# Reordering the seven products of a Strassen-Winograd multiplication, and multiplying by h straight from the accumulator

## The chip, the core and the metric

The kernel runs on one core of one Trainium2 chip. The metric is the device time of one execution in microseconds, as a median over runs; it includes what lies around the instructions of the program. The profile comes from one more execution under the hardware profiler. Its page gives the span from the first to the last instruction, and the times in the profile count from the start of that span.

## The reference

An attention block feeds a feed-forward block. For each of 8 batches, with 8 heads of 64 columns, 512 tokens read 32 states and the 32 states read the 512 tokens. The results of all batches are stacked into 4352 rows of 512 columns, and the feed-forward block turns each row into a row of 512 again, through 2048 hidden columns.

```python
scores = scale * np.matmul(x, state.transpose(0, 1, 3, 2))
a = softmax(scores);  xread = np.matmul(a, state)           # 512 rows a batch
scores2 = scale * np.matmul(state, x.transpose(0, 1, 3, 2))
a2 = softmax(scores2); sread = np.matmul(a2, x)             # 32 rows a batch
x = concatenate([xread, sread], axis=2) -> (4352, 512)
h = x @ w_in                                                # 512 x 2048
g = h * erf(softplus(h))
out = g @ w_out                                             # 2048 x 512
```

The two weights arrive as 64-bit numbers and are made into 32-bit ones on the chip.

## The kernel before

**The weights.** Each weight comes in 8 pieces (`i` for w_in, `o` for w_out). A piece is loaded as raw words into one of three buffers by a DMA of the SyncE queue, then ScalarE makes two steps of its conversion (L152, L154) and VectorE three (L155, L156, L157); the last VectorE step also issues the DMA of the third piece after it. This goes on through the whole first batch.

**The first batch.** For batch 0 the hidden columns are worked through in four groups g of 512 columns, each in four parts i of 128. `mixed_part` (L455) multiplies the states with a piece of w_in into m (copied from the accumulator by ScalarE, L457 and L458). `first0` (L828) multiplies m with the attention weights into a tile h of the accumulator, PSUM. h then goes two ways: `soft` (ScalarE, L832) writes softplus(h) into `gT[0]`, and `keep_h` (VectorE, L835) copies h into `gT[1]`. `erf` (ScalarE, L838) works on `gT[0]` in place, `times` (VectorE, L841) multiplies `gT[0]` with the copy in `gT[1]`, and `some0` or `by_halves` multiply the result with w_out (`project`, L626). ScalarE loads a new function table each time it goes from softplus to erf or exp and back.

[...] The pool `ps_h` holds two (tiles `h`), `ps_at` two (tiles `at`, used by `mixed_part`, by the scores and by transposes), `ps_o` four (tiles `o`, the sums of the second multiplication). A tile is given again only when its readers are done.

**The other batches.** Batches 1 to 7 are worked through in 14 turns n = 0 to 13, two for each batch b (u = 0 and 1, each for half of the hidden columns). Here each of the two multiplications of the feed-forward block is done as a 2 x 2 block product with seven multiplications instead of eight, with sums of blocks made before and after (Winograd's form). `hidden_wide` makes the first multiplication (L559, adds of VectorE in L542, copies of ScalarE in L565 and L574, softplus in L552). `erf_part` and `finish_on_act` (L1082, L616) and `times_part` (L1086) finish g. `sums_of` makes the sums S1 to S4 of its blocks on VectorE (L734, L735), and `combine_w` those of w_out, T1 to T4 (L652).

`project_wide` is the second multiplication, and the place of the first part of the change. One call of it is a pass: seven products, each four matmuls of 256 columns (the profile shows each matmul as two records, so a product has 8). It has two banks, p and q, in halves: a and d are the halves of p, c and e those of q. Before, the seven come in this order, with the adds of VectorE (L686) and the copies of ScalarE (L707, L719) between them:

| product | into | what follows it |
|---|---|---|
| A11 B11 | a | ScalarE copies a to m1 |
| S2 T2 | c | u2 = m1 + c |
| S1 T1 | d | v = u2 + d |
| S3 T3 | c, afresh | o2 = (u2, v) + (c, c) |
| A12 B21 | a, added to | ScalarE copies a to c11, a half of o1 |
| A22 T4 | e | c21 += e (a half of o2), o2 is stored |
| S4 B22 | d, afresh | c12 = v + d (a half of o1), o1 is stored |

A turn has two passes. The inner one runs by itself after the hidden stage of its turn. The outer one is kept as `pending`: its first half-products are laid between the products of the next turn's `hidden_wide`, which gives VectorE and ScalarE time there, and the rest follows that stage. A pass yields after each half of a product and after each product; the number k of the yield decides what else is put there. At k = 5 stands the excursion: reading the tokens of a batch (L285), the mixed weights of the next (`mixed_pair`, L442) and the scores of the one after (L205). `after` (the two `times_part` of the outer half) stands at k = 3, and in turns 4, 6, 8 and 10 the exps of the next batch's softmax (L388, L390 on ScalarE) stand at k = 5 too. `fill` and `rest` deal out smaller jobs of VectorE.

**The order.** Each engine works through its instructions in the order in which the program gives them, which is fixed by `in_order`. An instruction waits on semaphores until what it reads is there and what it overwrites has been read.

Of the kernel before, what the change touches and what calls it, by code (L numbers as in the profile page):

```python
# [9 lines left out]
F32 = mybir.dt.float32  # L10
U32 = mybir.dt.uint32
ALU = mybir.AluOpType
# [5 lines left out]
def kernel(  # L18
# [40 lines left out]
    outs = ctx.enter_context(tc.tile_pool(name="outs", bufs=2))  # L59
# [285 lines left out]
    def all_of(jobs):  # L345
        for f in jobs:
            f()
# [283 lines left out]

    def store(acc, put):
        for r in range(NC):
            ot = outs.tile([P, d_model], F32, name="ot")
            nc.scalar.copy(ot, acc[r])
            put(r, ot)

    E2 = d_model // 2
# [41 lines left out]
    def project_wide(n, g, put, more):  # L680
        gT, hs = slot(n)
        blocks = lambda t: [t[:, k].rearrange("p (i t) -> p i t", i=GF) for k in range(4)]
        A11, A21, A12, A22 = blocks(gT)
        S1, S2, S3, S4 = blocks(hs)
        tt = nc.vector.tensor_tensor
        add = lambda o, x, y: tt(o, x, y, op=ALU.add)  # L686
        half = n_acc[0] % 2
        n_acc[0] += 1
        p, q = (ps_o.tile([P, d_model], F32, name="o%d" % (2 * half + k)) for k in range(2))
        halves = lambda t: (t[:, 0:E2], t[:, E2:])  # L690
        (a, d), (c, e) = halves(p), halves(q)
        m1 = outs.tile([P, E2], F32, name="m1")
        uv = outs.tile([P, d_model], F32, name="uv")
        o1, o2 = (outs.tile([P, d_model], F32, name="ot") for _ in range(2))
        (c11, c12), (c21, c22), (u2, v) = halves(o1), halves(o2), halves(uv)
        two = lambda t: t.rearrange("p (c e) -> p c e", c=2)

        def product(lhs, rhs, out, start=False):
            for i in range(GF):
                if i == 2:  # L700
                    yield
                nc.tensor.matmul(out=out, lhsT=lhs[:, i, :], rhs=rhs[:, g, i, :],  # L702
                                 start=(start and i == 0), stop=(i == GF - 1),
                                 skip_group_check=not start)

        yield from product(A11, B11, a, True)
        nc.scalar.copy(m1, a)  # L707
        yield
        yield from product(S2, T[2], c, True)
        add(u2, m1, c)  # L710
        yield
        yield from product(S1, T[1], d)
        add(v, u2, d)
        yield
        yield from product(S3, T[3], c, True)
        add(two(o2), two(uv), c.unsqueeze(1).to_broadcast([P, 2, E2]))
        yield
        yield from product(A12, B21, a)
        nc.scalar.copy(c11, a)  # L719
        yield  # L720
        yield from product(A22, T[4], e)
        add(c21, c21, e)
        put(1, o2, more=more)
        yield
        yield from product(S4, B22, d, True)
        add(c12, v, d)
        put(0, o1, more=more)

    def sums_of(n):
# [9 lines left out]
    def store7(acc, put):  # L739
        twice = lambda t: t.unsqueeze(1).to_broadcast([P, 2, E2])  # L740
        two = lambda t: t.rearrange("p (c e) -> p c e", c=2)
        m1 = outs.tile([P, E2], F32, name="m1")
        u3 = outs.tile([P, d_model], F32, name="uv")[:, 0:E2]
        o1, o2 = (outs.tile([P, d_model], F32, name="ot") for _ in range(2))
# [34 lines left out]
    def begins(b):  # L779
        return 1 - b % 2  # L780
# [42 lines left out]
    h_t = {}  # L823

    def first0(g, i, gT):
        h = h_t[i] = ps_h.tile([P, S], F32, name="h")
        for e in range(2):
            nc.tensor.matmul(out=h, lhsT=m_t[0, g][:, e, P * i:P * i + P], rhs=aT[0][:, e],  # L828
                             start=(e == 0), stop=(e == 1))

    def soft(i, gT):
        nc.scalar.activation(out=gT[0][:, i], in_=h_t[i], func=ACTF.Softplus)  # L832

    def keep_h(i, gT):
        nc.vector.tensor_copy(gT[1][:, i], h_t[i])  # L835

    def erf(ks, gT):
        nc.scalar.activation(out=gT[0][:, ks], in_=gT[0][:, ks], func=ACTF.Erf)  # L838

    def times(ks, gT):  # L840
        nc.vector.tensor_tensor(gT[0][:, ks], gT[0][:, ks], gT[1][:, ks], op=ALU.mult)  # L841

    groups = [0]

# [27 lines left out]
    def some0(g, gT, rs, ts):  # L872
        done(project(gT[0], g, acc, rs, ts))

    def evict(i, gT, late=False):
        for f in (keep_h, soft) if late else (soft, keep_h):
            f(i, gT)
# [7 lines left out]
    keep_h(0, g0)  # L885
    on_dve("o", 0, [1])
    soft(1, g0)
    keep_h(1, g0)
    mixed_part(0, 0, 1, 2, nc.scalar.copy, nc.scalar.copy)
    on_dve("o", 0, [2])  # L890
    erf(A, g0)
# [1 line left out]
    on_act("o", 1)  # L893
    for i in 2, 3:
        first0(0, i, g0[0])
        evict(i, g0, True)
    erf(Z, g0)
    acc = tiles(NC)
    some0(0, g0, range(NC), range(2))
# [12 lines left out]
    g1 = group()  # L912
    first0(1, 0, g1[0])
    on_dve("o", 2, [0])
    evict(0, g1, True)
# [4 lines left out]
    evict(1, g1, True)  # L920
    on_act("o", 3, [1])
    on_dve("o", 3, [0])
    erf(A, g1)
    on_act("i", 4)
    first0(1, 2, g1[0])
    keep_h(2, g1)
    on_dve("o", 3, [1])
    first0(1, 3, g1[0])
    times(A, g1)
    keep_h(3, g1)  # L930
    on_dve("o", 3, [2])
    some0(0, g0, range(2, 3), range(3, 4))
    some0(0, g0, range(3, 4), range(2, 4))
# [16 lines left out]
    g2 = group()  # L950
    first0(2, 0, g2[0])
    on_dve("o", 4, [0, 1])
    evict(0, g2, True)
    mixed_part(0, 2, 1, 2, nc.scalar.copy, nc.scalar.copy)
    first0(2, 1, g2[0])
    on_act("o", 5, [0])
    evict(1, g2, True)
    on_dve("o", 4, [2])
    on_act("o", 5, [1])
    first0(2, 2, g2[0])  # L960
    evict(2, g2, True)
    on_dve("o", 5, [0])
    first0(2, 3, g2[0])
    evict(3, g2, True)
    on_dve("o", 5, [1])
    some0(1, g1, range(1, 4), range(2, 4))

# [30 lines left out]
    mixed_part(0, 3, 1, 2, nc.scalar.copy, nc.scalar.copy)  # L998
    first0(3, 1, g3[0])
    soft(1, g3)  # L1000
    all_of(most[:6])
    for i in 0, 1:
        keep_h(i, g3)
    all_of(most[6:])
    exps()
    on_dve("o", 6, [2])
# [1 line left out]
    some0(2, g2, range(1, 2), range(2, 4))  # L1008
    for i in 2, 3:
        first0(3, i, g3[0])  # L1010
        evict(i, g3)
    some0(2, g2, range(2, 3), range(2, 4))
    finish_(g3)
    mixed(1, 2 * begins(1), nc.scalar.copy, nc.scalar.copy)
    some0(2, g2, range(3, 4), range(2, 4))
    all_of(ready[:4])
    on_act("o", 7)
# [6 lines left out]
    def by_halves():  # L1024
        yield from project(g3[0], 3, acc, range(NC), range(2))
        for r in range(NC):
            yield from project(g3[0], 3, acc, range(r, r + 1), range(2, 4))
            ot = outs.tile([P, d_model], F32, name="ot")
            nc.scalar.copy(ot, acc[r])
            put_x(0, r // 2)(r % 2, ot)  # L1030

# [62 lines left out]
    for n, (b, u) in enumerate((b, u) for b in range(1, B) for u in range(2)):  # L1094
# [45 lines left out]
        for k, _ in enumerate(steps):  # L1140
            k += 6
            if k == 6:
                fill(1.2)
            if k == 7:
                fill(1.2)
            if k == 8 and n == 2:
                excursion(2, m_next, 3)
                bring(1 - begins(b + 1))
            if k == 9:
                break  # L1150
# [30 lines left out]
        def rest(n):  # L1181
            for _ in range(min(n, len(more))):
                more.popleft()()

        for k, _ in enumerate(project_wide(inner, o, put[1 - low], u)):
            if k == 0:
                all_of(sums[3:])
                fill(0.6)
            if k == 3:
                all_of(after)  # L1190
            if k == 4:
                fill(99)
            if k == 5 and n != 2:
                if b == 1:
                    excursion(m=m_next)
                elif u == 0:
                    excursion(m=m_next)
                else:
                    excursion(b + 1 if b + 1 < B else None, m_next, b + 2 if b + 2 < B else None)
                if u == 0 and b + 1 < B:  # L1200
                    bring(1 - begins(b + 1))
                if b == B - 1 and u == 0:
                    for i in range(0, B, 4):
                        turn_read(range(i, min(i + 4, B)))
                if steady and u == 0 and b + 1 < B:
                    soft[b + 1][1]()
            rest({5: 1 if n == 2 or b == B - 1 else 4 if u else 3, 6: 1, 7: 0, 8: 2, 9: 1, 10: 2, 11: 1, 12: 1}.get(k, 0))
        if n > 1:
            rest(99)
# [60 lines left out]
```

## Time and profile before

| | |
|---|---|
| time, median of 3 runs (lowest to highest) | 729.69 us (729.67 to 730.13) |
| time of the profiled execution | 729.88 us |
| its span | 728.0 us |
| TensorE, matmuls: busy | 716.6 us, 98% |
| TensorE, weight loads: busy | 562.0 us, 77% |
| VectorE busy | 546.0 us, 75% |
| ScalarE busy | 370.1 us, 51% |
| granted clock of TensorE | 1.000 |
| share of the chain that ended last: TensorE, ScalarE, VectorE | 80%, 4%, 3% |
| copies of h in the first batch (L835) | 16, 685 ns each |
| multiplications by the copy (L841) | 4 of 1024 columns, 1223 ns; 8 of 512 columns, 685 ns |
| adds of the seven products (L686) | 112 of 256 columns, 415 to 421 ns; 28 of 512, 680 ns |
| copies of the seven products (L707, L719) | 28 and 28, 364 and 361 ns |

A row of the timeline has the start and the duration in us, the engine, the line, the operation, the tiles written and read, and how many records are merged in it; the brackets say how long the engine had been idle and what released it. PE is TensorE, PEld its weight loads, DVE VectorE, ACT ScalarE, POOL GpSimd, SPq the DMA queue of SyncE. In the table by stage the columns after each pair of times are the busy times of PE, PEld, DVE, ACT and POOL with their instructions, then the granted clock, the DMA share and GB/s. Matmuls overlap in the pipeline, so that their busy times say less than the distance between their starts.

### The profile page before, as it was taken

The page shows a single profiled execution, that of the slowest core. Times are in us where ns is not written, and L with a number is a line of the kernel's source. Part 1 is how long each engine was busy: PE and PEld are TensorE (multiplying, and loading weights), DVE is VectorE, ACT ScalarE, POOL GpSimd, SP SyncE. Part 2 cuts the span into 40 slices and gives each one's busy share as a digit, 9 for nine tenths or more (in the row PEclk, how much of TensorE's full clock was granted, in tenths as well). Part 3 has the DMA queues.
Part 4 walks back from the last instruction along what each step waited for, and adds up shares of the span by engine and source line. Part 5 has one row for each costly group of instructions (what it writes and reads, how often), then busy time and mean ns, then how long its engine had stood idle before and what let it go on. Part 6 is the DMA issues. An engine that isn't in the chain of part 4 may idle for free.

```text
span 728.0 us, 10875 instructions
## 1 busy us (share of the span) xinstructions
PE 716.6 (98%) x4232; PEld 562.0 (77%) x4232; DVE 546.0 (75%) x872; ACT 370.1 (51%) x536; POOL 25.2 (3%) x34
## 2 busy tenths in 40 slices
PE   8899999999999999999999999999999999999997
PEld 7434436588778878887888878787888888889996
DVE  4988899788868998678776867698777756765533
ACT  4898894536354534645345526453464434342340
POOL 0000000000100000000000000000000000000000
PEclk9999999999999999999999999999999999999999
DMA  7587786560239154422714270614232231102201
GB/s 235 175 244 216 217 235 232 145 181 30 38 65 215 48 123 65 98 86 67 128 18 155 54 138 14 174 26 128 50 81 102 71 67 19 40 30 30 23 7 29
DMA packets 142907, 74.64 MB, mean 103 GB/s; under 512 B 127112, under 2 KB 127368, under 8 KB 141320
## 3 DMA queue, kind: packets, MB, share of 16 engines
q1 hardware_dynamic: 136552, 65.89, 32.8%
q0 software_dynamic: 4032, 7.34, 7.6%
q10 hardware_dynamic: 2272, 0.72, 0.5%
q8 instruction: 33, 0.54, 0.3%
q14 instruction: 18, 0.15, 0.1%
HBM read 49.81 MB, written 20.45 MB: 97 GB/s over the span
## 4 chain that ended last, share of the span: by engine, by line
PE 80%; ACT 4%; DVE 3%; issue 1%; ACTq 0%; DVEq 0%
PE o L702 44%; PE h L559 13%; PE at L559 10%; PE h L604 3%; PE o L676 3%; PE h L442 2%; PE at L442 1%; ACT xT L390 1%; PE at L285 1%; PE o L626 1%; PE h L205 1%; DVE ring L1086 0%; DVE w_out L156 0%; ACT ring L838 0%; ACT ring L1082 0%
## 5 line engine op out<-in xcount | busy, mean ns | idle before, releaser
L702 PE MATMUL o<-w_out,ring 128*128 128x256 f32 x896 | 209.5, 381 | 0.4
L702 PEld LDWEIGHTS o<-w_out,ring 128*128 128x128 f32 x896 | 168.4, 190 | 35.6 <-DVE uv L686 5.5
L702 PE MATMUL o<-raw,ring 128*128 128x256 f32 x672 | 161.3, 380 | 1.3 <-DVE ring L734 0.7
L702 PEld LDWEIGHTS o<-raw,ring 128*128 128x128 f32 x672 | 127.1, 190 | 19.9 <-issue 1.1
L552 ACT ACTIVATE ring<-ring 128x512 f32<-128x512 f32 x112 | 70.6, 631 | 61.5 <-DVE ring L542 60.9
L1086 DVE TENSOR_TENSOR ring<-ring 128x1024 f32<-128x1024 f32 x60 | 71.8, 1221 | 20.9 <-ACT ring L1082 16.9
L559 PE MATMUL h<-aT,m 128*128 128x256 f32 x336 | 82.2, 380 | 0.1
L559 PEld LDWEIGHTS h<-aT,m 128*128 128x128 f32 x336 | 63.5, 190 | 11.0 <-DVE ring L542 1.2
L542 DVE TENSOR_TENSOR ring<-ring,at 128x512 f32<-128x512 f32 x84 | 57.0, 679 | 14.8 <-PE at L559 13.1
L626 PE MATMUL o<-w_out,ring 128*128 128x512 f32 x128 | 59.0, 599 | 0.6 <-DVE ring L841 0.5
L542 DVE TENSOR_TENSOR ring<-ring,h 128x512 f32<-128x512 f32 x56 | 37.9, 676 | 22.8 <-PE h L559 21.0
L686 DVE TENSOR_TENSOR ot<-uv,o 128x512 f32<-128x512 f32 (+1 forms) x56 | 30.7, 549 | 27.2 <-PE o L702 24.7
L565 ACT COPY ring<-h 128x512 f32<-128x512 f32 x28 | 16.4, 586 | 64.0 <-PE h L559 64.0
L762 POOL DMA_DIRECT2D out_dram<-ot x28 | 24.5, 936 | 663.4 <-DVE ot L686 663.4
L626 PEld LDWEIGHTS o<-w_out,ring 128*128 128x128 f32 x128 | 23.5, 190 | 29.4 <-issue 24.4
L574 ACT COPY ring<-h 128x512 f32<-128x512 f32 x28 | 16.4, 588 | 47.0 <-PE h L559 47.0
L734 DVE TENSOR_TENSOR ring<-ring 128x512 f32<-128x512 f32 x56 | 38.6, 689 | 1.4
L735 DVE TENSOR_TENSOR ring<-ring 128x512 f32<-128x512 f32 x56 | 36.2, 683 | 0.0
L828 PE MATMUL h<-aT,m 128*128 128x512 f32 x64 | 29.8, 604 | 1.0 <-ACT m L457 0.5
L616 ACT ACTIVATE ring<-ring 128x2048 f32<-128x2048 f32 x16 | 30.5, 1905 | 0.0
L444 ACT COPY m<-h 128x512 f32<-128x512 f32 x11 | 6.4, 586 | 46.7 <-PE h L442 46.7
L1082 ACT ACTIVATE ring<-ring 128x1024 f32<-128x1024 f32 x28 | 29.6, 1059 | 0.2
(180 smaller groups left out, 955.4 us busy)
## 6 DMA issues: line engine op xcount, KB each, us to landing
w_in<-kept_in SPq DMA_DIRECT2D x7, 2048.0 KB, 8.5
raw<-in_moe_w_in_dram SPq DMA_DIRECT2D x8, 1024.0 KB, 5.7
raw<-in_moe_w_out_dram SPq DMA_DIRECT2D x8, 1024.0 KB, 4.9
out_dram<-ot SPq DMA_DIRECT2D x32, 256.0 KB, 2.2
xq<-in_x_dram SPq DMA_DIRECT2D x112, 64.0 KB, 2.3
x<-in_x_dram SPq DMA_DIRECT2D x56, 128.0 KB, 2.8
out_dram<-ot POOLq DMA_DIRECT2D x28, 256.0 KB, 4.5
sc<-xT SPq DMA_DIRECT2D x112, 32.0 KB, 1.9
```

Of the source, the lines that this page charges most:

```text
L542: add = lambda o, x, y: nc.vector.tensor_tensor(o, x, y, op=ALU.add)
L552: nc.scalar.activation(out=s[k], in_=hs[k], func=ACTF.Softplus)
L559: nc.tensor.matmul(out=out[:, i], lhsT=x[:, q:q + P], rhs=y, start=(first and i == 0), stop=(i == 1), skip_group_check=not first)
L616: nc.scalar.activation(out=s, in_=s, func=ACTF.Erf)
L626: nc.tensor.matmul(out=acc[r], lhsT=gT[:, i, P * r:P * r + P], rhs=w_out[:, GF * g + i, :], start=(g == 0 and i == 0), stop=(g == NG - 1 a ...
L686: add = lambda o, x, y: tt(o, x, y, op=ALU.add)
L702: nc.tensor.matmul(out=out, lhsT=lhs[:, i, :], rhs=rhs[:, g, i, :], start=(start and i == 0), stop=(i == GF - 1), skip_group_check=not start)
L734: return [lambda: tt(S1, A21, A22, op=ALU.add), lambda: tt(S2, S1, A11, op=ALU.subtract), lambda: tt(S3, A11, A21, op=ALU.subtract), lambd ...
L735: lambda: tt(S3, A11, A21, op=ALU.subtract), lambda: tt(S4, A12, S2, op=ALU.subtract)]
L828: nc.tensor.matmul(out=h, lhsT=m_t[0, g][:, e, P * i:P * i + P], rhs=aT[0][:, e], start=(e == 0), stop=(e == 1))
L1082: nc.scalar.activation(out=s[:, ks], in_=s[:, ks], func=ACTF.Erf)
L1086: nc.vector.tensor_tensor(s[:, ks], s[:, ks], hs[:, ks], op=ALU.mult)
```

## The change

First, the seven products of `project_wide` stand in another order, and two sums are formed in another way. A22 T4 becomes the second product. S3 T3 is added to S2 T2 in the accumulator and S4 B22 to S1 T1, where both started afresh before. A12 B21 and the copy of c11 close the pass. c12 is begun already after S2 T2, in the output tile. m1 moves into the tile `uv`, and the output tiles `ot` have three buffers instead of two. Some numbers k move with it: the exps of the later turns to k = 7, the excursion of turn 2 to k = 7 of its pending pass, and in turn 2 six steps of the next softmax stand at k = 3 and `after` at k = 10.

Second, in the first batch `keep_h` is gone: h stays in PSUM until `times` multiplies with it, one part i at a time. The third and fourth h of a group are tiles of `ps_at`. The first `mixed` of batch 1 moves from behind group 3's erf to ahead of the softmax steps of batch 1.

```diff
@@ store, project_wide
-        m1 = outs.tile([P, E2], F32, name="m1")
         uv = outs.tile([P, d_model], F32, name="uv")
-        o1, o2 = (outs.tile([P, d_model], F32, name="ot") for _ in range(2))
-        (c11, c12), (c21, c22), (u2, v) = halves(o1), halves(o2), halves(uv)
+        o1, o2 = (outs.tile([P, d_model], F32, name="ot", bufs=3) for _ in range(2))
+        (c11, c12), (c21, c22), (m1, v) = halves(o1), halves(o2), halves(uv)
...
         yield from product(A11, B11, a, True)
         nc.scalar.copy(m1, a)
         yield
-        yield from product(S2, T[2], c, True)
-        add(u2, m1, c)
+        yield from product(A22, T[4], e, True)
+        yield
+        yield from product(S2, T[2], c)
+        add(c12, m1, c)
         yield
         yield from product(S1, T[1], d)
-        add(v, u2, d)
+        add(v, m1, d)
         yield
-        yield from product(S3, T[3], c, True)
+        yield from product(S3, T[3], c)
         add(two(o2), two(uv), c.unsqueeze(1).to_broadcast([P, 2, E2]))
         yield
+        yield from product(S4, B22, d)
+        yield
         yield from product(A12, B21, a)
-        nc.scalar.copy(c11, a)
-        yield
-        yield from product(A22, T[4], e)
         add(c21, c21, e)
         put(1, o2, more=more)
-        yield
-        yield from product(S4, B22, d, True)
-        add(c12, v, d)
+        nc.scalar.copy(c11, a)
+        add(c12, c12, d)
         put(0, o1, more=more)
@@ the first batch
     def first0(g, i, gT):
-        h = h_t[i] = ps_h.tile([P, S], F32, name="h")
+        pool, name = ((ps_h, "h"), (ps_at, "at"))[i // 2]
+        h = h_t[i] = pool.tile([P, S], F32, name=name)
...
-    def keep_h(i, gT):
-        nc.vector.tensor_copy(gT[1][:, i], h_t[i])
-
     def times(ks, gT):
-        nc.vector.tensor_tensor(gT[0][:, ks], gT[0][:, ks], gT[1][:, ks], op=ALU.mult)
+        for i in range(ks.start, ks.stop):
+            nc.vector.tensor_tensor(gT[0][:, i], gT[0][:, i], h_t[i], op=ALU.mult)
...
     soft(1, g3)
+    mixed(1, 2 * begins(1), nc.scalar.copy, nc.scalar.copy)
     all_of(most[:6])
-    for i in 0, 1:
-        keep_h(i, g3)
     all_of(most[6:])
     exps()
...
     finish_(g3)
-    mixed(1, 2 * begins(1), nc.scalar.copy, nc.scalar.copy)
     some0(2, g2, range(3, 4), range(2, 4))
@@ the turns
-            if k == 8 and n == 2:
+            if k == 7 and n == 2:
                 excursion(2, m_next, 3)
...
             if k == 3:
+                if n == 2:
+                    rest(6)
+                else:
+                    all_of(after)
+            if k == 10 and n == 2:
                 all_of(after)
...
-                if steady and u == 0 and b + 1 < B:
-                    soft[b + 1][1]()
+            if k == 7 and steady and u == 0 and b + 1 < B:
+                soft[b + 1][1]()
```

More of the change, by code (lines that the diff above doesn't have):

```diff
@@ L633, in store @@
         for r in range(NC):
-            ot = outs.tile([P, d_model], F32, name="ot")
+            ot = outs.tile([P, d_model], F32, name="ot", bufs=3)
             nc.scalar.copy(ot, acc[r])
@@ L741, in store7 @@
         two = lambda t: t.rearrange("p (c e) -> p c e", c=2)
-        m1 = outs.tile([P, E2], F32, name="m1")
-        u3 = outs.tile([P, d_model], F32, name="uv")[:, 0:E2]
-        o1, o2 = (outs.tile([P, d_model], F32, name="ot") for _ in range(2))
+        uv = outs.tile([P, d_model], F32, name="uv")
+        m1, u3 = uv[:, 0:E2], uv[:, E2:]
+        o1, o2 = (outs.tile([P, d_model], F32, name="ot", bufs=3) for _ in range(2))
         c12 = o1[:, E2:]
@@ L873, in some0 @@
         done(project(gT[0], g, acc, rs, ts))
-    def evict(i, gT, late=False):
-        for f in (keep_h, soft) if late else (soft, keep_h):
-            f(i, gT)
     first0(0, 0, g0[0])
@@ L884 @@
     on_dve("o", 0, [0])
-    keep_h(0, g0)
     on_dve("o", 0, [1])
     soft(1, g0)
-    keep_h(1, g0)
     mixed_part(0, 0, 1, 2, nc.scalar.copy, nc.scalar.copy)
@@ L895 @@
         first0(0, i, g0[0])
-        evict(i, g0, True)
+        soft(i, g0)
     erf(Z, g0)
@@ L914 @@
     on_dve("o", 2, [0])
-    evict(0, g1, True)
+    soft(0, g1)
     mixed_part(0, 1, 1, 2, nc.scalar.copy, nc.scalar.copy)
@@ L919 @@
     on_act("o", 3, [0])
-    evict(1, g1, True)
+    soft(1, g1)
     on_act("o", 3, [1])
@@ L925 @@
     first0(1, 2, g1[0])
-    keep_h(2, g1)
     on_dve("o", 3, [1])
@@ L929 @@
     times(A, g1)
-    keep_h(3, g1)
     on_dve("o", 3, [2])
@@ L952 @@
     on_dve("o", 4, [0, 1])
-    evict(0, g2, True)
+    soft(0, g2)
     mixed_part(0, 2, 1, 2, nc.scalar.copy, nc.scalar.copy)
@@ L956 @@
     on_act("o", 5, [0])
-    evict(1, g2, True)
+    soft(1, g2)
     on_dve("o", 4, [2])
@@ L960 @@
     first0(2, 2, g2[0])
-    evict(2, g2, True)
+    soft(2, g2)
     on_dve("o", 5, [0])
     first0(2, 3, g2[0])
-    evict(3, g2, True)
+    soft(3, g2)
     on_dve("o", 5, [1])
@@ L1010 @@
         first0(3, i, g3[0])
-        evict(i, g3)
+        soft(i, g3)
     some0(2, g2, range(2, 3), range(2, 4))
     finish_(g3)
-    mixed(1, 2 * begins(1), nc.scalar.copy, nc.scalar.copy)
     some0(2, g2, range(3, 4), range(2, 4))
@@ L1027, in by_halves @@
             yield from project(g3[0], 3, acc, range(r, r + 1), range(2, 4))
-            ot = outs.tile([P, d_model], F32, name="ot")
+            ot = outs.tile([P, d_model], F32, name="ot", bufs=3)
             nc.scalar.copy(ot, acc[r])
```

## The prediction

> **What bounds the kernel now.** I read the page's busy shares first, then the table by stage, then TensorE's timeline with the other engines beside it, since the question is where TensorE is late.
>
> ```profile
> PE 716.6 (98%) x4232; PEld 562.0 (77%) x4232; DVE 546.0 (75%) x872; ACT 370.1 (51%) x536; POOL 25.2 (3%) x34
> ...
> 25.00:113.00 88.00, 86.59 (x409) 35.48 (x408) 76.67 (x102) 76.43 (x102) 0.00 (x0) 1.00 0.79 231
> 350.00:389.00 39.00, 39.00 (x204) 32.70 (x202) 27.94 (x45) 20.54 (x32) 3.48 (x4) 1.00 0.45 89
> ```
>
> TensorE has work in flight nearly always, at full clock, so only its lost time can be won, not its work. In the first batch (25 to 113) VectorE and ScalarE are each busy 76 of 88 us too: there a wait on either reaches TensorE. Lost time is read from start to start, because the busy figure of a pipelined engine hides it. One product of the second multiplication is 8 records.
>
> ```profile
> 373.10 1.89 PE L702 MATMUL o<-raw,ring 128*128 128x256 f32 x8
> ...
> 374.82 3.62 PE L702 MATMUL o<-w_out,ring 128*128 128x256 f32 x16
> ...
> 387.26 1.89 PE L702 MATMUL o<-raw,ring 128*128 128x256 f32 x8
> ...
> 388.82 0.35 ACT L719 COPY ot<-o 128x256 f32<-128x256 f32 x1
> ...
> 389.22 1.59 PEld L702 LDWEIGHTS o<-w_out,ring 128*128 128x128 f32 x8 [0.48 <-ACT ot L719]
> 389.22 1.99 PE L702 MATMUL o<-w_out,ring 128*128 128x256 f32 x8
> ...
> 391.05 1.03 PE L559 MATMUL h<-aT,m 128*128 128x256 f32 x4
> ```
>
> Undisturbed, a product takes 374.82 - 373.10 = 1.72 us. A22T4 at 387.26 took 1.96 and S4B22 at 389.22 took 1.83: 0.23 and 0.10 lost, because S4B22 writes the bank from which ScalarE copies c11 (L719), and that copy stood behind the exps of the next batch until 388.82. The same pair (1.96, 1.83) stands at 308.11, 466.41 and 545.56.
>
> ```profile
> 137.25 1.99 PE L702 MATMUL o<-w_out,ring 128*128 128x256 f32 x8
> 139.92 3.69 PE L702 MATMUL o<-raw,ring 128*128 128x256 f32 x16 [0.68 <-DVE ring L734]
> ...
> 178.33 1.89 PE L702 MATMUL o<-raw,ring 128*128 128x256 f32 x8
> 180.81 1.99 PE L702 MATMUL o<-raw,ring 128*128 128x256 f32 x8 [0.58 <-ACT m L707]
> 182.73 1.09 PE L442 MATMUL h<-w_in,st 64*32 64x512 f32 x16
> ...
> 655.32 3.98 PE L702 MATMUL o<-w_out,ring 128*128 128x256 f32 x16
> 659.23 1.99 PE L702 MATMUL o<-raw,ring 128*128 128x256 f32 x8
> ```
>
> Turn 0: A11B11 to S2T2 is 2.67, so 0.95 is lost to the sum S2 (L734). Turn 1: 2.48, so 0.75 is lost to the copy m1 (L707), which stood behind exps. Turn 13: two products took 3.91 instead of 3.45.
>
> ```profile
> 45.56 0.60 ACT L832 ACTIVATE ring<-h 128x512 f32<-128x512 f32 x1 [0.41 <-DVE ring L835]
> 48.55 0.60 ACT L832 ACTIVATE ring<-h 128x512 f32<-128x512 f32 x1 [0.61 <-DVE ring L835]
> 49.20 1.98 PE L828 MATMUL h<-aT,m 128*128 128x512 f32 x4 [0.18 <-ACT ring L832]
> ...
> 94.77 0.60 ACT L832 ACTIVATE ring<-h 128x512 f32<-128x512 f32 x1 [0.83 <-PE h L828]
> ...
> 103.48 2.19 ACT L838 ACTIVATE ring<-ring 128x512 f32<-128x512 f32 x4
> ...
> 104.89 1.98 PE L626 MATMUL o<-w_out,ring 128*128 128x512 f32 x4 [0.25 <-DVE ring L841]
> ```
>
> In the first batch Softplus waits for VectorE's copy of h, and the third and fourth h wait for the banks of the first two.
>
> **The change, part 1: the order of the seven products.** Work is the same: 7 products, 5 VectorE adds, 2 ScalarE copies in a pass, and SP's and POOL's queues keep their order. What moves is who waits. In the built program's order the waits per pass are by bank: before, S3T3, A12B21 and A22T4 each wait for a VectorE add and S4B22 for ScalarE's c11, mostly one product behind its reader, A22T4 and S4B22 with one or two. After, S1T1 waits for m1 (two products and the excursion lie between), S3T3 for the add c12 and S4B22 for the add v (one product each); A12B21 and the c11 copy close the pass, and no product of the pass waits for that copy.
>
> Turn 0: A22T4 (1.73) now runs while S2 is made (ready at 139.78; S2T2 would start at 140.7): +0.95. Turn 1: m1 ends at 180.76, S1T1 starts after 181.8: +0.75; the exposed weight loads that go with the waits (180.81, 184.61 and 188.26 each 0.10 long): +0.30. The four even turns: 4 x (0.23 + 0.10) = +1.32. Turn 13: S4B22 waits for v instead of A12B21; v moves ahead of two sums and would end at 657.6, S4B22 starts at 658.8: +0.46 + 0.10 = +0.56.
>
> What is late next: v. In the outer passes it stands behind L542 and two L469 and would end 0.8 us before S4B22; in turns 0 and 1 by 0.3 and 0.1; I cost these at nothing while that cover lasts, and each 0.1 beyond it at 0.1. Turn 2 is where it fails: six softmax steps (L376, L378, L380, 3.9 us in all by their rows) now come ahead of c12 instead of the two times-steps (2.4 us). I get c12 ending at 227.3 against a start of S3T3 at 227.1: -0.25. The third ot buffer: o2 needs the store of the pass before, as before, and at the same fifth product; the add of c12, two products earlier than the c11 copy was, now meets the buffer of two passes before, issued a pass or some 20 us earlier. Nothing.
>
> **Part 2: h left in the accumulator.** Gone: 16 copies of 685 ns (L835), 10.7 us of VectorE. Four multiplications of 1223 and eight of 685 (9.9 us) become 16 that read h from PSUM. No row shows that product; nearest are L542, with one PSUM operand, at 676 to 679, and L734, without, at 689: I take 0.68, both ends within 0.01: 10.9 us, so VectorE is freed of 9.7. [...] Either way it falls beside waits: sum unchanged.
>
> Walking groups 0 to 2 with the rows' own durations: the third and fourth h no longer wait for the first banks (at 26.95 saves 0.3, but the piece of w_in that is ready at 40.99 caps it at 0.3); Softplus starts 0.7 and 1.25 earlier at 45.56 and 48.55; one record of 512 columns takes 0.429 (24 of L626 from 71.75 to 82.05), so the 12 of L828 from 45.32 to 51.02 lost 0.55 and the 22 of L626 from there to 60.92 lost 0.46; of both some 0.9 goes. TensorE is then 1.2 us ahead, to 94.5.
>
> There the moved `mixed` takes it back. Its two copies (L457, L458; 0.56 and 0.58 in the later place) and the wait for its matmuls now stand ahead of the table load and exps: from 95.39 to 96.65 is 1.26, less the 0.42 that the exps waited for L384. Softplus of 2 and 3, and erf (103.48), come 0.9 later; TensorE, which no longer has that `mixed` to do there, waits at g3's projection from about 104.1 to 105.8 where it now starts at 104.89. So -0.95, and the first batch nets +0.25.
>
> [...] Here four banks are held until erf times h. Their next users are the `mixed_part` matmuls (L455). At 60.92 they followed group 1's last multiplication (60.66) by 0.26. By my walk both come 1.2 earlier and still fit, by 0.2. If erf did not move, TensorE would wait 1.0 there: first batch -0.75, sum 2.9 instead of 3.9. I follow the rows, since the Softplus waits that hold erf back are what is removed.
>
> **Sum.** 0.95 + 1.05 + 1.32 + 0.56 - 0.25 + 0.25 = 3.9 us. The profiled execution has a span of 728.0 and a time of 729.88, 0.19 over the median 729.69. Span 724.1, time 729.69 - 3.9 = 725.8.
>
> **The rivals.** (a) The first batch costs more than it gives: the 0.95 is sure and the 1.2 is not (TensorE held at L455). Then -1.0 to -0.5 there, sum 2.6 to 3.1, 726.6 to 727.1. For it: slack of 0.2. (b) The moved `mixed` finds room, exps being ahead already: 0.9 more, 724.9, and the small losses at 234 to 249 (0.4) may go too: 724.5. Against it: the 0.83 wait at 94.77 shows ScalarE level with TensorE there. (c) Slower: VectorE's queue makes S4B22 wait for v in every pass. Price: slack is 0.8 in the 14 outer and about 1.1 in the inner passes; if v came 1.1 later than I place it, 14 x 0.3 = 4.2 us, plus 1.0 and 0.8 in turns 0 and 1, sum -2.1: 731.8. It decides from about 1.0 us of lateness. Against it: inside hidden stages VectorE has lost the u2 add. (d) The waits removed leave the same loss elsewhere, as TensorE then meets the first VectorE result of the next hidden stage earlier: no change, 729 to 730. Against it: no loss at L559 in steady turns.
>
> **How the numbers follow.** Forecast 0.60, (a) 0.16, (b) 0.12, (c) 0.06, (d) 0.06. A difference under 0.2% (1.5 us) can't be told from none. Faster 0.87, within 0.07, slower 0.06. The range takes (a), (b) and the bounds of the first batch: 723.9 to 727.8.
>
> **What would show it.** Right: no c11 wait of weight loads in the even turns, S2T2 right behind A22T4 in turn 0, S1T1 unheld in turn 1; g3's projection waiting about 1.7 us for erf near 104; a small wait at S3T3 in turn 2. Wrong: L702 rows over 1.73 per product that wait for L686; L455 waiting for the multiplications; TensorE reaching the first L559 of batch 1 later than 113.07.

## The result, and the profile after

The changed kernel takes 725.57 us (median of four runs, 725.28 to 726.43) against 729.78 for the kernel before beside it. The ratio is 0.9944, with a 95% interval of 0.9926 to 0.9961. Run again later beside other kernels it took 725.75 (725.39 to 726.11) against 729.85, ratio 0.9943 (0.9931 to 0.9956). The forecast was 725.8.

The page first: the span is 723.4 us, and the profiled execution took 725.28, 0.3 under its own median.

```profile
PE 713.4 (99%) x4232; PEld 564.1 (78%) x4232; DVE 537.2 (74%) x860; ACT 372.2 (51%) x536; POOL 25.2 (3%) x34
...
PE 93%; ACT 3%; DVE 2%; DMA 1%; issue 0%; ACTq 0%; DVEq 0%
```

The first line is the busy times, the second the engines' shares of the chain that ended last. TensorE has the same 4232 matmuls, and holds 93% of the chain where it held 80%. VectorE is busy 8.8 us less, and only the first batch shows it (76.67 before, 67.95 after, by the table by stage for 25 to 113 us). ScalarE is no less busy there, and the steady stage is as it was:

```profile
25.00:113.00 88.00, 85.87 (x410) 35.89 (x409) 67.95 (x91) 76.54 (x102) 0.00 (x0) 1.00 0.78 232
...
350.00:389.00 39.00, 39.00 (x205) 32.91 (x204) 28.45 (x46) 21.10 (x34) 2.62 (x3) 1.00 0.44 103
```

TensorE's timeline, at the places that the prediction named:

```profile
136.95 1.99 PE L701 MATMUL o<-w_out,ring 128*128 128x256 f32 x8
138.78 3.62 PE L701 MATMUL o<-raw,ring 128*128 128x256 f32 x16
...
177.11 3.62 PE L701 MATMUL o<-raw,ring 128*128 128x256 f32 x16
180.66 1.09 PE L442 MATMUL h<-w_in,st 64*32 64x512 f32 x16
...
303.83 5.34 PE L701 MATMUL o<-w_out,ring 128*128 128x256 f32 x24
309.01 1.03 PE L559 MATMUL h<-aT,m 128*128 128x256 f32 x4
...
653.02 5.34 PE L701 MATMUL o<-w_out,ring 128*128 128x256 f32 x24
658.20 1.95 PE L604 MATMUL h<-sT,w_in 128*128 128x128 f32 x16
```

Turn 0: the two products from 136.95 start 1.83 apart, 0.10 over one product, and no release is named. Turn 1: 16 records in 3.55. Turn 4: the last three products in 309.01 - 303.83 = 5.18, three times 1.73, with nothing lost. Turn 13: 5.18 too. The waits of these four places are gone, those for S2, m1, c11 and, in turn 13, v.

Where TensorE was when, by the start of the first record of each stage:

| | before | after | lead |
|---|---|---|---|
| first L559 of batch 1 | 113.07 | 112.97 | 0.10 |
| inner pass of turn 0 | 137.25 | 136.95 | 0.30 |
| outer pass of turn 0 | 154.16 | 152.94 | 1.22 |
| inner pass of turn 1 | 176.61 | 175.39 | 1.22 |
| outer pass of turn 1 | 193.55 | 191.28 | 2.27 |
| outer pass of turn 2 | 234.08 | 231.93 | 2.15 |
| inner pass of turn 3 | 256.93 | 254.38 | 2.55 |
| outer pass of turn 10 | 551.08 | 547.16 | 3.92 |
| inner pass of turn 13 | 650.14 | 646.11 | 4.03 |
| end of the last matmul | 724.22 | 719.64 | 4.59 |

Turn 0 gave 0.92 in its inner pass, turn 1 1.05, turns 4 to 10 together 1.37, turn 13 0.56. Turn 2 lost 0.12 in its inner pass and won 0.40 in the hidden stage behind it, which the prediction had in a rival and not in its sum. Turn 0's hidden stage won 0.20 (one row of L626 and the next of L559 start 1.11 apart before, at 115.75, and 0.91 after, at 115.65), and 0.11 lies between turns 10 and 13; the prediction has neither. The last matmul ends 4.59 us earlier; the medians moved 4.2, as the profiled execution of before was 0.1 over its median here and that of after 0.3 under its own. The first batch gave 0.10, no more than two traces of the old first batch differ by (in `order_only` below TensorE is at the first L559 at 112.94). It has a new wait, here by the timeline of all engines:

```profile
102.09 1.28 ACT L835 ACT_TABLE_LOAD   x1
...
103.38 2.19 ACT L835 ACTIVATE ring<-ring 128x512 f32<-128x512 f32 x4
104.04 1.28 DVE L839 TENSOR_TENSOR ring<-ring,h 128x512 f32<-128x512 f32 x2 [3.97 <-ACT ring L835]
...
104.79 1.13 PE L626 MATMUL o<-w_out,ring 128*128 128x512 f32 x2 [1.37 <-DVE ring L839]
```

Erf of group 3 starts at 103.38, 0.10 before where it was, and TensorE, which had been over a microsecond ahead, stands 1.37 us in front of group 3's projection.

### The profile page after: what moved, and what is told of

Its sections match the earlier page's. It is cut to its first block, busy times and chain, and to the rows that moved or that the text cites. A ratio compares the mean times of both kernels' runs of the same rounds, so it can differ in the third digit from the quotient of the medians.

```text
span 723.4 us, 10832 instructions
## 1 busy us (share of the span) xinstructions
PE 713.4 (99%) x4232; PEld 564.1 (78%) x4232; DVE 537.2 (74%) x860; ACT 372.2 (51%) x536; POOL 25.2 (3%) x34
## 4 chain that ended last, share of the span: by engine, by line
PE 93%; ACT 3%; DVE 2%; DMA 1%; issue 0%; ACTq 0%; DVEq 0%
PE o L701 47%; PE h L559 13%; PE at L559 10%; PE o L626 6%; PE h L604 3%; PE o L676 3%; PE h L828 2%; PE h L442 2%; PE at L442 1%; PE at L285 1%; PE at L828 1%; PE at L455 1%; DMA x<-in_x_dram 1%; PE h L205 1%; ACT L835 1%; PE at L205 0%
## 5 line engine op out<-in xcount | busy, mean ns | idle before, releaser
L701 PE MATMUL o<-w_out,ring 128*128 128x256 f32 x896 | 203.0, 379 | 0.0
L559 PE MATMUL h<-aT,m 128*128 128x256 f32 x336 | 82.0, 380 | 0.0
L559 PEld LDWEIGHTS h<-aT,m 128*128 128x128 f32 x336 | 63.7, 190 | 10.4 <-DVE ring L542 0.7
L626 PE MATMUL o<-w_out,ring 128*128 128x512 f32 x128 | 58.5, 597 | 1.4 <-DVE ring L839 1.4
L686 DVE TENSOR_TENSOR ot<-uv,o 128x256 f32<-128x256 f32 (+1 forms) x56 | 30.9, 552 | 30.5 <-PE o L701 28.4
L724 ACT COPY ot<-o 128x256 f32<-128x256 f32 x28 | 10.4, 372 | 79.7 <-PE o L701 79.7
L626 PEld LDWEIGHTS o<-w_out,ring 128*128 128x128 f32 x128 | 23.7, 190 | 29.4 <-issue 24.2
L686 DVE TENSOR_TENSOR ot<-ot,o 128x256 f32<-128x256 f32 x56 | 22.1, 416 | 27.9 <-ACT ot L724 27.7
L733 DVE TENSOR_TENSOR ring<-ring 128x512 f32<-128x512 f32 x56 | 38.6, 689 | 1.4
L565 ACT COPY ring<-h 128x512 f32<-128x512 f32 x28 | 16.4, 586 | 28.3 <-PE h L559 28.3
```

What stands on the lines that cost most here:

```text
L559: nc.tensor.matmul(out=out[:, i], lhsT=x[:, q:q + P], rhs=y, start=(first and i == 0), stop=(i == 1), skip_group_check=not first)
L626: nc.tensor.matmul(out=acc[r], lhsT=gT[:, i, P * r:P * r + P], rhs=w_out[:, GF * g + i, :], start=(g == 0 and i == 0), stop=(g == NG - 1 a ...
L733: return [lambda: tt(S1, A21, A22, op=ALU.add), lambda: tt(S2, S1, A11, op=ALU.subtract), lambda: tt(S3, A11, A21, op=ALU.subtract), lambd ...
```

## The experiments

**The two parts apart.** `order_only` is the kernel before with the reordering and all numbers k that go with it; `h_only` is the kernel before with the first batch's edits, the earlier `mixed` among them. No run has the new order with two `ot` buffers, so the third one has not been tried apart.

> The second multiplication's new order alone, with the first batch as it was. Theory (the two parts add, and the order carries nearly all): the wait for S2 in turn 0, for m1 in turn 1, for c11 in turns 4, 6, 8 and 10 and for v in turn 13 go as in the changed kernel; the two traces read 4.3 us for everything behind 131 us, so 729.7 - 4.3 = 725.4, and by the prediction's own terms (0.95 + 1.05 + 1.32 + 0.56 - 0.25 = 3.6) 726.1. Rival 1 (the first batch brought more than the two traces show at 131 us, because VectorE and ScalarE come out of it earlier and turn 0 lives on that): turn 0 keeps a wait, 727 to 728. Rival 2 (the order needs the freed VectorE): no gain, 729.5.

Measured: 725.54 (725.43 to 725.86), ratio 0.9942 (0.9930 to 0.9955).

> The first batch's h left in the accumulator (with the earlier place of mixed that goes with it), with the seven products in the old order. Theory (TensorE gets 1.2 us ahead by 94.5 us, and the moved mixed gives back nearly all, as erf of group 3 starts where it did): the gain is 0.1 to 0.3 us, 729.4 to 729.6, with the last four records of L626 near 104.8 waiting 1.4 us for the multiplications. Rival (VectorE's freed 9.7 us carries on into turn 0 and takes away the wait for S2 there): 728.6.

Measured: 730.02 (729.37 to 730.61), ratio 1.0002 (0.9994 to 1.0010). So the reordering is the whole gain: by medians 729.74 - 725.54 = 4.20. The second part is worth nothing that can be told from zero, alone or on top of the first. Its theory holds in the trace of `h_only`: the same wait for the multiplications stands in TensorE's timeline, with the old waits of turn 0 behind it.

```profile
104.96 1.98 PE L626 MATMUL o<-w_out,ring 128*128 128x512 f32 x4 [1.37 <-DVE ring L840]
```

The runs of `h_only` spread more than those of any kernel without the second part; the experiment on erf below shows a likely cause.

**Who takes the lead of the first batch.** `vcopy` has VectorE make the two copies of the moved `mixed`, behind the softmax steps:

```diff
-    mixed(1, 2 * begins(1), nc.scalar.copy, nc.scalar.copy)
-    all_of(most[:6])
-    all_of(most[6:])
+    all_of(most)
+    mixed(1, 2 * begins(1), nc.vector.tensor_copy, nc.vector.tensor_copy)
     exps()
```

> The changed kernel, with the two copies of the moved mixed (L457, L458) taken by VectorE behind the whole of most, instead of by ScalarE ahead of exps. Theory (these copies and the wait for their matmuls are what keeps erf of group 3 where it was): the table load of exps starts at 94.3 instead of 95.8, erf of group 3 at 102.1 instead of 103.4, and the wait of 1.4 us at group 3's projection is nearly gone: 725.6 - 1.3 = 724.3. Rival 1 (something behind erf holds that place: the multiplications or a weight conversion on VectorE, which the two copies delay by 1.3): gain 0.3 at most, 725.3 to 725.6. Rival 2 (the gain is lost again in turn 0, where TensorE would meet other late results): 725.6.

Measured: 724.29 (724.02 to 724.71), ratio 0.9925 (0.9913 to 0.9938), the fastest version with the one below. Its timeline:

```profile
94.53 1.28 ACT L388 ACT_TABLE_LOAD   x1
...
96.01 0.68 DVE L457 COPY m<-at 128x512 f32<-128x512 f32 x1
96.61 0.68 DVE L458 COPY m<-at 128x512 f32<-128x512 f32 x1
...
102.39 2.19 ACT L835 ACTIVATE ring<-ring 128x512 f32<-128x512 f32 x4
```

The changed kernel, at the same place:

```profile
94.73 0.58 ACT L457 COPY m<-at 128x512 f32<-128x512 f32 x1 [0.47 <-PE at L455]
...
95.82 1.28 ACT L388 ACT_TABLE_LOAD   x1
```

The table load of the exps (L388) starts at 94.53 instead of 95.82, erf follows at 102.39 instead of 103.38, and TensorE starts the first L559 of batch 1 at 111.99 instead of 112.97. The two copies on ScalarE, 1.1 us in all, and its wait of 0.47 for the matmuls that they copy had taken the lead.

**Why `mixed` had to move at all.** `mixed_back` is the changed kernel with `mixed` put behind `finish_(g3)` again, where the kernel before has it.

```diff
     soft(1, g3)
-    mixed(1, 2 * begins(1), nc.scalar.copy, nc.scalar.copy)
...
     finish_(g3)
+    mixed(1, 2 * begins(1), nc.scalar.copy, nc.scalar.copy)
```

> The changed kernel, with mixed put back behind finish_ of group 3, where the kernel before has it. Theory (h in four banks is what forces the earlier place): erf of group 3 starts near 102.1 instead of 103.4, but mixed needs the two banks of the third and fourth h, which are held until the last multiplication at about 104.9; TensorE comes to it at 100.5 and waits about 4.4 us, so about 2.6 us are lost against the changed kernel: 728.2 (727.7 to 728.5), with L455 near 105 waiting for L839. Rival (the earlier place is a loss that nothing forces): erf comes 1.3 earlier and TensorE does mixed in the gap, 724.3 to 724.7.

Measured: 730.58 (730.03 to 732.01), ratio 1.0011 (1.0003 to 1.0020). The wait is as foretold, and the loss is twice as large. First the timeline, then the table by stage (the granted clock is the third number from the end):

```profile
102.12 2.19 ACT L835 ACTIVATE ring<-ring 128x512 f32<-128x512 f32 x4
...
104.72 2.55 PE L455 MATMUL at<-w_in,st 64*32 64x512 f32 x16 [3.95 <-DVE ring L839]
...
107.20 5.35 PE L626 MATMUL o<-w_out,ring 128*128 128x512 f32 x8
```

```profile
96.00:100.50 4.50, 4.50 (x12) 1.79 (x10) 3.19 (x8) 4.47 (x9) 0.00 (x0) 1.00 0.72 117
100.50:104.70 4.20, 0.27 (x1) 0.00 (x0) 1.92 (x4) 3.78 (x6) 0.00 (x0) 0.88 0.97 312
104.70:107.20 2.50, 2.48 (x16) 0.41 (x17) 2.50 (x5) 0.00 (x0) 0.00 (x0) 0.50 0.98 419
107.20:110.60 3.40, 3.40 (x11) 1.51 (x5) 1.17 (x2) 3.13 (x4) 0.00 (x0) 0.51 1.00 414
110.60:113.00 2.40, 2.40 (x21) 0.75 (x19) 0.00 (x0) 0.00 (x0) 0.00 (x0) 1.00 0.69 287
```

L455 waits 3.95 us for the multiplications that hold the banks (a bank is the place of one tile `h` or `at`). During that wait TensorE's clock falls to 0.50 and stays there for about 6 us from the wait's end: from start to start the 16 records of L455 take 2.48 instead of 1.02, and the eight of L626 5.28 instead of 3.43. That is 3.3 us on top of the wait; at most 0.6 of it is L455's second wait, for the bank of the fourth h (up to 105.31).

**Turn 2.** `turn2_back` undoes what the change does there:

```diff
             if k == 3:
-                if n == 2:
-                    rest(6)
-                else:
-                    all_of(after)
-            if k == 10 and n == 2:
                 all_of(after)
```

> The changed kernel, with turn 2 as every other turn: the two times-steps at the fourth half product and the softmax steps behind, instead of six softmax steps there. Theory (the prediction's own term: the six steps make S3T3 wait 0.25 for c12): without them 0.25 comes back, 725.3. Rival (the trace after shows no such wait, and the four small losses of 0.39 in the hidden stage at 234 to 249 are gone: the six steps took them away): without them the 0.39 returns, 726.0, with waits at L559 between 230 and 250.

Measured: 728.52 (727.60 to 730.49), ratio 0.9986 (0.9980 to 0.9993), 3 us slower than the changed kernel: neither theory has the time. The timelines of `turn2_back`, of the kernel before and of the changed kernel:

```profile
230.25 0.17 DVE L384 TENSOR_SCALAR m<-m 128x2 f32<-128x2 f32 x1
...
230.97 1.28 ACT L388 ACT_TABLE_LOAD   x1
...
234.73 0.56 ACT L565 COPY ring<-h 128x512 f32<-128x512 f32 x1
...
235.35 1.99 PE L559 MATMUL h<-aT,m 128*128 128x256 f32 x8 [2.21 <-ACT ring L565]
```

```profile
234.31 0.56 ACT L565 COPY ring<-h 128x512 f32<-128x512 f32 x1
```

```profile
223.96 1.23 ACT L388 ACTIVATE xT<-xT 128x512 f32<-128x512 f32 x2 [2.43 <-DVE xT L380]
224.45 0.41 DVE L686 TENSOR_TENSOR ot<-uv,o 128x256 f32<-128x256 f32 x1
...
224.92 5.04 PEld L701 LDWEIGHTS o<-w_out,ring 128*128 128x128 f32 x24 [0.31 <-DVE ot L686]
...
231.26 0.58 ACT L565 COPY ring<-h 128x512 f32<-128x512 f32 x1 [0.49 <-PE h L559]
```

Exps is the last item of the list in which the softmax steps stand, and on ScalarE it stands ahead of the hidden stage's first copy (L565). With the six early steps it comes ahead of the copy c11 that closes the pass, at 223.96. Without them the softmax is ready at 230.4, exps stands behind c11 and starts at 230.97, the copy L565 comes at 234.73, and TensorE waits 2.21 us for it at 235.35. In the kernel before, L565 came at 234.31, and it had cost little, since TensorE itself came 2 us later to that place. The changed kernel has the copy at 231.26. So without the six steps TensorE gives back in this one place about the 2.27 us that turns 0 and 1 had won. The clock may come in again: of the 21 runs nine at a granted clock of 0.997 or 0.998 took 729.16 to 730.49, and twelve at 0.999 or 1.000 took 727.60 to 729.04, with a median of 728.06, 2.5 over the changed kernel.

The wait at S3T3 that the first theory takes from the prediction does exist: in the changed kernel the weight load at 224.92 waited for the add c12 above it, and S3T3 comes 0.08 late and takes 0.10 more, 0.18 in all. In `turn2_back` the same weight load waits for nothing. The second theory's sentence that the trace shows no such wait is wrong; it stands in the row of the weight load and not in that of the matmuls.

**The exps in the steady turns, and in turn 1.** `exps_late` is the kernel before with one line moved:

```diff
-                if steady and u == 0 and b + 1 < B:
-                    soft[b + 1][1]()
+            if k == 9 and steady and u == 0 and b + 1 < B:
+                soft[b + 1][1]()
```

> The kernel before, with one line moved: in the steady even turns exps of the next batch is issued behind the copy c11 (at the tenth half product) instead of ahead of it. Theory (c11 late behind exps is the whole loss of the even turns): 4 x (0.23 + 0.10) = 1.3 us, 728.4, and A22T4 and S4B22 take 1.73 each. Rival (exps then delays the sums z, or ScalarE's first work of the next hidden stage, by about 4 us, and TensorE waits there): 729.7 or slower, with a wait at L559 behind the pass.

Measured: 728.44 (728.24 to 728.72), ratio 0.9982 (0.9975 to 0.9989). In the trace A22T4 and S4B22 of turn 6 now take 1.72 and 1.73:

```profile
386.85 1.89 PE L702 MATMUL o<-raw,ring 128*128 128x256 f32 x8
388.57 1.89 PE L702 MATMUL o<-w_out,ring 128*128 128x256 f32 x8
390.30 1.03 PE L559 MATMUL h<-aT,m 128*128 128x256 f32 x4
```

`exps_late1` does the same for turn 1:

```diff
-        if n == 1:
-            soft[2][1]()
         all_of(sums[2:3])
...
+            if k == 1 and n == 1:
+                soft[2][1]()
             if k == 3:
```

> The kernel before, with one line moved in turn 1: exps of batch 2 is issued behind the copy m1 of the inner pass instead of ahead of it. Theory (turn 1 lost 0.75 only because m1 stood behind exps on ScalarE, as the prediction has it): m1 ends near 178.9 instead of 180.8, S1T1 starts at 180.06, and 0.75 to 1.05 of the prediction's term for turn 1 comes without any reordering of the products: 728.7 to 729.0. Rival (the sums z behind exps, or the copies L444 behind it on ScalarE, then become the wait): 729.5 to 730.

Measured: 729.40 (729.24 to 729.63) against 729.85, ratio 0.9993 (0.9985 to 1.0002): 0.45 of the 0.75 to 1.05. The interval takes in 1, but all 13 runs lie below all 17 of the kernel before (from 729.69 on). Its timeline tells where the rest is:

```profile
178.44 3.62 PE L702 MATMUL o<-raw,ring 128*128 128x256 f32 x16
...
183.86 3.72 PE L702 MATMUL o<-w_out,ring 128*128 128x256 f32 x16
187.92 1.99 PE L702 MATMUL o<-raw,ring 128*128 128x256 f32 x8 [0.33 <-DVE ot L686]
```

S1T1 follows S2T2 at once, as expected; but in the old order the next product (A22T4, at 187.92) then waits for the add of o2, which stands behind L401 on VectorE. The rows from 183.86 to 187.92 are 4.06 for two products, 0.60 over. In turn 1 one moved line takes away the wait for m1, and of the two ways tried only the new order keeps all of the gain.

**How late v may be.** `late_v2` and `late_v4` make the add v three and five times over in the changed kernel, with the same result (the diff of the first; the second has 5):

```diff
-        add(v, m1, d)
+        for _ in range(3):
+            add(v, m1, d)
```

> The changed kernel, with the add v made three times in place of once (the same result), so that v ends 2 x 0.32 = 0.64 us later in each of the 28 passes. In the trace after, v ends 1.0 to 1.1 before S4B22 in the steady passes, 0.70 before it in turn 0, 0.34 in turn 1 and 0.37 in turn 2 (inner passes). Theory (v is what S4B22 waits for, and this slack is the cover): only turns 1 and 2 lose, 0.3 each, and with 0.1 for each exposed weight load 0.8 in all: 726.4 (726.0 to 726.8). Rival (v is not on TensorE's path, c12 or the banks are): 725.6.

Measured: 728.59 (728.12 to 732.23), ratio 0.9987 (0.9980 to 0.9993).

> The same with the add v made five times: v ends 4 x 0.32 = 1.28 us later. Theory: the steady passes lose 1.28 - 1.10 = 0.18 each, those with a slack of 0.96 to 0.98 0.32, and 0.15 each for the exposed weight load and the wait's own time; 20 x 0.33 + 4 x 0.47 + turns 0, 1 and 2 with 0.7, 1.1 and 1.05 = 11.3: 737 (734 to 739). That is the mechanism of the prediction's slower rival, with its threshold of about 1.0 us. Rival (the lateness is taken up by TensorE's order, or another engine covers it): below 730.

Measured: 754.88 (753.46 to 755.20), ratio 1.0340 (1.0326 to 1.0354). The direction is right, the sizes are not. VectorE's and TensorE's rows of `late_v4` show why:

```profile
300.68 2.24 DVE L686 TENSOR_TENSOR uv<-uv,o 128x256 f32<-128x256 f32 x5 [1.04 <-PE o L701]
```

```profile
300.48 1.89 PE L701 MATMUL o<-w_out,ring 128*128 128x256 f32 x8
302.97 5.45 PE L701 MATMUL o<-w_out,ring 128*128 128x256 f32 x24 [0.60 <-DVE uv L686]
```

Five adds to the same tile end 2.24 after the first starts, so they start 0.455 apart, where others of their size start 0.33 apart: the delays were 0.91 and 1.82. With these, the theory's own arithmetic holds. At 1.82 a steady pass is 1.82 - 1.10 = 0.72 late, and its fifth and sixth product stood 0.77 further apart in 20 of the 28 passes, and some 0.9 in the four with the shorter slack. These, 5.1 in the inner passes of turns 0 to 2, 0.1 for each weight load that waited, and some 1.5 that a lower clock cost in turn 1 (the last section has its rows) make 28 of the 29 us.

At 0.91 only the four passes with the shorter slack lost anything from turn 3 on, 0.1 each, an exposed weight load. With that load in each, turn 0 lost 0.36, turn 2 0.70, turn 1 1.57. In turn 1 the changed kernel's VectorE shows no idle time between the outer pass's v, which lies in its hidden stage, and the inner pass's, so the outer one hands its 0.91 on too: 0.91 + 0.91 - 0.34 = 1.48, and the weight load. Together that is the 3.0 measured.

**The banks in the first batch.** `vcopy_split` is `vcopy` with this:

```diff
-    erf(Z, g1)
+    erf(slice(2, 3), g1)
+    erf(slice(3, 4), g1)
```

> The version with the copies of the moved mixed on VectorE, and with one more edit: erf of group 1's third and fourth block is issued as two instructions instead of one. It is about the prediction's rival (a), TensorE held at L455 near 60 us because the third and fourth h are held until the multiplications: that wait was 0 in the trace after, but 0.3 to 0.6 in the traces of the kernels that share this first batch. Theory (it is that wait, and it hangs on the one erf of 1.06 us): the first multiplication starts 0.5 earlier, the wait goes, 724.3 - 0.3 = 724.0. Rival (VectorE or a weight conversion sets when these multiplications start): 724.3.

> The changed kernel once more, unchanged, beside the other two on one chip: how far the wait at L455 near 60 us, and with it the time, varies from run to run and chip to chip. Expected: median 725.3 to 725.9, the wait 0 to 0.6.

Measured: `vcopy_split` 724.33 (724.17 to 725.01), ratio 0.9926 (0.9914 to 0.9938); `after_again` as given at the top. The rows of L455 near 60 us, in the changed kernel's first trace, in that of `after_again` and in that of `vcopy_split`:

```profile
59.80 0.66 PE L455 MATMUL at<-ring,st 64*32 64x256 f32 x16
```

```profile
59.84 1.16 PE L455 MATMUL at<-ring,st 64*32 64x256 f32 x16
60.94 1.98 PE L626 MATMUL o<-w_out,ring 128*128 128x512 f32 x4
```

```profile
59.90 0.66 PE L455 MATMUL at<-ring,st 64*32 64x256 f32 x16
```

In one trace of the changed kernel there is no wait there, in the other L455 takes 0.5 longer: the bank of the fourth h is held until its multiplication is done. The two traces of the changed kernel differ by 0.5 at the end (spans of 723.4 and 724.0), and nearly all of it arises here. Splitting erf removes the wait, and the time does not move, since TensorE's transposes (L190) come at 62.46 as they do in `vcopy` (62.47). In the trace of `vcopy_split` their weight load waited 0.82 for ScalarE's copy L457 (62.05 to 62.40), which stands behind the weight step L152 (60.98 to 62.15). So the theory is right about the wait (the first multiplication starts at 58.22, in `vcopy` at 58.72) and wrong about the time, as the next thing that TensorE needs comes no earlier. Moving that weight step was not tried.

## Why the prediction was right

**Turn 0, turn 1, the even turns and turn 13** came as written: 0.92 for 0.95, 1.05 for 1.05, 1.37 for 1.32, 0.56 for 0.56. For the even turns `exps_late` shows the cause by itself: 729.74 - 728.44 = 1.30. For turn 1 `exps_late1` shows the cause, and that removing it alone trades it for another wait. Turns 0 and 13 rest on the two traces and on that of `order_only`, which has both gains with the first batch as it was.

**The term of turn 2** had its mechanism right and its size a little high: S3T3 waits for c12 and loses 0.18, forecast 0.25. The pass as a whole is 0.12 slower, as the old one had lost 0.06 at A22T4 (1.79 from 228.84 to 230.63). But the prediction asked only what the six steps delay. What it left out is what they bring forward: exps, and behind exps on ScalarE the first copy of the next hidden stage. That stage is 0.40 faster, and without the six steps the kernel takes 2.5 to 3 us more, which would have left the forecast's range. That is the mechanism of rival (d), a wait that turns up in the next hidden stage, and it was there, in one turn, with the six steps against it. The prediction did not know that they were needed; that the change had them is luck for the forecast.

**The first batch** netted 0.10 for the forecast 0.25 in the trace, and nothing by medians (725.57 and 725.75 with the second part, 725.54 in `order_only` without it). The 0.20 in turn 0's hidden stage comes with it too: the rows that start 0.91 apart in the changed kernel do so in `h_only` (0.92), and in `order_only` they start 1.12 apart. So the second part wins 0.3 in a good execution, and the wait near 60 us takes 0.55 in `after_again` (L626 at 60.94 for 60.39). The mechanism was right at both ends: TensorE was 1.1 us ahead (the scores, L205, start at 87.16 where they started at 88.28), and the moved `mixed` took it back at the place named, with a wait of 1.37 for the forecast 1.7. The prediction's times for that wait, 104.1 to 105.8, are those of the old timeline; less its own lead of 1.2 they are 102.9 to 104.6, and its sum fits these. Measured were 103.42 to 104.79. `vcopy` shows the taker, ScalarE's two copies with the wait ahead of them. What rival (a) said also happened: the slack of 0.2 at L455 is as thin as it was called, and turns into a wait of 0.5 in `after_again`.

**The multiplications from the accumulator** (L839) took 684 and 681 ns, with both operands in SBUF (L733) 689: the 0.68 us that the prediction took for each was right. VectorE was freed of 8.8 us and not 9.7: the prediction subtracted 16 durations (10.9; their busy time is 10.2) from busy times of the old groups (10.7 and 9.9), and instructions that follow each other overlap a little. No term of the sum rests on it.

**Rival (c)**, v late in every pass, did not happen, and it was placed well: the slack is 1.10 in most passes and 0.96 in some, where the prediction had 0.8 and 1.1, and 0.70 and 0.34 in turns 0 and 1 for 0.3 and 0.1. A delay of 1.82 costs 29 us where 0.91 costs 3.

**The sum** was 3.9, the traces moved 4.59 and the medians 4.2. In the traces, 0.40 from the hidden stage behind turn 2 and 0.31 in two small places were left out, 0.13 too much was charged to turn 2's pass, and 0.15 too much was credited to the first batch: 3.88 + 0.40 + 0.31 + 0.13 - 0.15 is 4.57. That the forecast came within 0.3 of the medians owes something to misses of both signs.

## What to carry to other kernels

When a step is moved, ask what it brings forward as well as what it delays, down to the queue of the other engine behind it: the six steps of turn 2 were priced as a loss of 0.25 and are worth 2.5 to 3. In the first batch, where another engine is busy 76 of 88 us, TensorE's lead was worth only what that engine's own queue gained by the same place; follow such a queue to the next result TensorE needs. And a wait that is removed alone may be taken up by the next operand in line, as in `exps_late1`, so read the second-latest arrival before pricing the first.

## What the runs showed of the hardware

A wait of TensorE can cost more than its length. After 3.95 us of waiting in `mixed_back` the granted clock was 0.50 for some 6 us, and about 3 us were lost beyond the wait. In turn 1 of `late_v4` 2.25 us of waiting for v, up to 190.90, were followed by about 3.4 us at 0.50, from just before 192 on (the row of the wait and the table by stage are below), while 2.21 us in turn 2 of `turn2_back` left the clock at 1.00 in every microsecond from 232 to 239. What tells the two short waits apart, no run shows.

```profile
190.90 5.41 PE L701 MATMUL o<-w_out,ring 128*128 128x256 f32 x16 [2.25 <-DVE uv L686]
```

```profile
191.00:192.00 1.00, 1.00 (x5) 0.90 (x6) 1.00 (x3) 0.00 (x0) 0.00 (x0) 0.98 0.00 0
192.00:193.00 1.00, 1.00 (x4) 0.78 (x3) 0.96 (x4) 0.00 (x0) 0.00 (x0) 0.50 0.00 0
193.00:194.00 1.00, 1.00 (x4) 0.78 (x3) 1.00 (x3) 0.00 (x0) 0.00 (x0) 0.50 0.00 0
194.00:195.00 1.00, 1.00 (x4) 0.82 (x3) 0.42 (x2) 0.00 (x0) 0.26 (x1) 0.50 0.00 0
195.00:196.00 1.00, 1.00 (x5) 0.83 (x5) 0.00 (x0) 0.00 (x0) 0.75 (x1) 0.82 0.00 0
```

And VectorE's adds of 128 x 256 start 0.455 us apart in `late_v4` when each overwrites the last one's tile; four in a row of which none overwrites the last one's tile start 0.34, 0.34 and 0.33 apart there (L495, L496, L497 and L686, from 192.99 on).
